# A hand-written step order and its engine assignment exchanged for another, in a polysketch attention kernel with a multiplicative feed-forward part

## The chip, the cores and the metric

The kernel runs on one core of one Trainium2 chip. The metric is the device time of one execution in microseconds; the time of a kernel is the median of several runs. Short names of the engines: PE is TensorE (its weight loads are PEld), DVE is VectorE, ACT is ScalarE, POOL is GpSimd, SP is SyncE, which issues nearly all transfers.

## The reference

Polysketch attention, linear in the length of the sequence, and behind it a feed-forward part without a non-linearity other than a product:

```python
def phi(x):                                   # x: (4, 4, 1088, 32), S1, S2: (8, 32)
    a = np.einsum('rd,bhsd->bhsr', S1, x)
    b = np.einsum('rd,bhsd->bhsr', S2, x)
    return np.einsum('bhsi,bhsj->bhsij', a, b).reshape(*x.shape[:-1], 64)
q_p, k_p = phi(q), phi(k)
kv = np.einsum('bhsf,bhsd->bhfd', k_p, v)
z = np.sum(k_p, axis=2)
num = np.einsum('bhsf,bhfd->bhsd', q_p, kv)
den = np.einsum('bhsf,bhf->bhs', q_p, z)[..., None] + 1e-06
x = (num / den).astype(np.float32)            # -> (4352 tokens, 128)
h = (x @ w1) * (x @ w2) @ w3                  # w1, w2: (128, 1024), w3: (1024, 1024)
out = (h @ w_out).astype(np.float32)          # w_out: (1024, 128)
```

The inputs come as 64-bit floats, of which the kernel takes the words apart itself.

## The kernel before

The work is cut into about a thousand small steps, each a function under a name; one step issues one or a few instructions. A string `ORDER` lists all names. The entry function calls the steps in that order and chains, on every engine, each instruction behind the one before it. So each engine runs its instructions exactly in the order of the string, and waits where an input of the next one isn't there. Nothing overtakes on an engine. Steps whose names end in `.load` are transfers; each bulk one also waits until the fourth one before it has landed.

Four more tables belong to it. `SLOTS` names for every tile the buffer it gets: `b` are the 8 PSUM banks, `m`, `l`, `s` and others are buffers in SBUF. A tile waits until the one that had its buffer before is read for the last time. `POOL` is the set of steps that run on GpSimd instead of DVE, and `CPV` the set of copies out of PSUM that run on DVE instead of ACT. `WARM` gives the sizes of the filler steps `warm0` to `warm11`: matmuls on a tile of zeros (L255, tile idle_ps) that compute nothing.

The names of the steps that the text speaks of:

- `s.*` prepare the sketch matrices (`s.Pp`: four 32x32 operations on P, L409 to L412).
- `w0.*`, `w1.*` convert the two halves of w1 and w2 to 32-bit values; `w3` to `w10` are rows of w3, `f0` to `f7` fold w3 with w_out into one matrix, once for all tokens (L534).
- `k0` to `k3` are the keys of the four batches. `lead` and `rest` split k into two summands, tile kk (L214 and L651). `gram0` to `gram4` multiply k with itself on PE (L659, tile ps_g); `G*`, `T*`, `N*` make a scaling from it; `kp` is the feature map (L677), `kv*` the sums over the sequence.
- `q0` to `q3` are the halves of the queries of batches 0 and 1, `q4` and `q6` all of batches 2 and 3, `qr` the rest of 64 positions. A q part ends in `xc`, `xT` (L1274, L1291): the attention's output, transposed, which the feed-forward part reads.
- `g0.0a` to `g3.7o` are the feed-forward part of q0 to q3: for each of 8 chunks of d_ff two products `a`, `b` on PE (L1799, L1809, 128x512), a copy `c`, a product `m` on DVE (L1815), and the output product `o` (L1835). `gr.*` is the same for qr.
- `h4.*` and `h6.*` are the feed-forward part of q4 and q6 by a seven-product scheme: products of 64 rows (L1673), `h4.0a1` to `h4.3b7`, those with `a` on rows 0 to 63 of the array, those with `b` on rows 64 to 127 (`tile_position`). Sums `m11` to `m22`, `T1` to `T4` follow, then products `P1` to `P7` (L1759) and their sums `k1` to `k9`.
- `oT`, `oS`, `st` transpose, finish and store the output; `gr.st1` is the last store.

PE has products of the feed-forward part to do for most of the time, and the steps of attention lie between them in the string. Until q0's xT is ready, PE has attention work only.

## Time and profile before

| | before |
|---|---|
| time, median of 3 runs | 245.06 us (244.8, 245.06, 246.78) |
| span of the profiled execution | 244.1 us |
| PE, DVE, POOL, ACT busy | 97%, 85%, 66%, 51% |
| granted clock of PE | full in all 40 slices |
| transfers | 22.06 MB, 90 GB/s in the mean |

The page gives the busy time of each engine over the whole span, then in 40 slices. For a kernel whose one engine is busy 97% of the span, the shares tell little: what matters is the stretches in which that engine is not busy. The span of 244.1 us is the only time known of the profiled execution itself; the median of the runs is 0.96 us above it.

### The profile page before, as it was taken

What the parts mean: (1) busy time and instruction counts of PE and PEld (TensorE: products, weight loads), DVE (VectorE), ACT (ScalarE), POOL (GpSimd) and SP (SyncE); (2) the same over time, 40 slices, a digit from 0 to 9 for tenths busy, and PEclk for the clock granted to TensorE, in tenths of its full rate; (3) what the DMA queues carried; (4) which work ended last, traced back from release to release, by engine and by line L of the source; (5) the groups of instructions that cost most, each with busy time, mean ns of one, the idle gap of its engine ahead of it and who ended that gap; (6) DMA issues with size and microseconds to landing.
All of it is one profiled execution on the core that took longest, in us unless ns stands there. A gap on an engine that the chain in (4) does not pass through costs nothing.

```text
span 244.1 us, 6745 instructions
## 1 busy us (share of the span) xinstructions
PE 236.2 (97%) x2724; PEld 129.8 (53%) x2724; DVE 206.7 (85%) x421; ACT 123.5 (51%) x246; POOL 161.9 (66%) x203
## 2 busy tenths in 40 slices
PE   8998999899999999999999999999999999999994
PEld 5887454545545646766566444444443354463363
DVE  2876988999899998997899878498989789999792
ACT  3976957675666764593012914355651164730010
POOL 4576658344856998764583889929999425883670
PEclk9999999999999999999999999999999999999999
DMA  7959797078859897200000000360000000000054
GB/s 201 265 143 325 181 227 190 6 197 224 220 141 251 188 217 190 59 1 3 3 0 0 4 0 3 59 113 3 1 0 0 0 3 0 0 1 3 12 90 93
DMA packets 31935, 22.06 MB, mean 90 GB/s; under 512 B 21280, under 2 KB 26528, under 8 KB 31904
## 3 DMA queue, kind: packets, MB, share of 16 engines
q1 hardware_dynamic: 31360, 21.11, 35.1%
q8 instruction: 21, 0.34, 0.6%
q10 hardware_dynamic: 544, 0.52, 0.6%
q14 instruction: 10, 0.08, 0.1%
HBM read 19.40 MB, written 2.23 MB: 89 GB/s over the span
## 4 chain that ended last, share of the span: by engine, by line
PE 87%; DMA 5%; ACT 2%; POOL 2%; DVE 1%; issue 1%; POOLq 0%; SPq 0%
PE b_ps L1809 12%; PE ps_o L1835 12%; PE ps_X L1673 11%; PE a_ps L1799 11%; PE ps_o L1759 10%; PE ps_w3o L534 6%; PE ps_Y L1673 6%; PE ps_Z L1673 3%; PE ps_g L659 2%; PE ps_x L1527 2%; PE ps_ac L1374 2%; DMA qh<-in_q_dram 2%; DMA k<-in_k_dram 2%; PE ps_or L1824 2%; POOL ph L1208 1%; PE idle_ps L255 1%
## 5 line engine op out<-in xcount | busy, mean ns | idle before, releaser
L1673 PE MATMUL ps_X<-xd,wv 64*128 64x512 f32 x112 | 36.3, 593 | 0.0
L1799 PE MATMUL a_ps<-xT,w 128*128 128x512 f32 (+1 forms) x80 | 36.1, 562 | 0.0
L1809 PE MATMUL b_ps<-xT,w 128*128 128x512 f32 (+1 forms) x80 | 35.6, 555 | 0.0
L1804 ACT COPY ffa<-a_ps 128x512 f32<-128x512 f32 (+1 forms) x38 | 20.1, 540 | 29.2 <-PE a_ps L1799 26.7
L1707 POOL TENSOR_TENSOR hc<-hc 128x512 f32<-128x512 f32 x16 | 20.7, 1304 | 15.7 <-DVE hc L1685 15.5
L1835 PE MATMUL ps_o<-ab,w3o 128*128 128x512 f32 x64 | 29.6, 600 | 0.0
L1680 ACT COPY hc<-ps_X 128x512 f32<-128x512 f32 x38 | 21.3, 590 | 16.1 <-PE ps_X L1673 12.9
L1815 DVE TENSOR_TENSOR ab<-ffa,b_ps 128x512 f32<-128x512 f32 (+1 forms) x40 | 23.9, 623 | 4.9 <-PE b_ps L1809 4.1
L501 POOL TENSOR_TENSOR w3c<-w3c,cv_m 128x512 int32<-128x512 int32 x16 | 21.2, 1344 | 4.2 <-DVE w3c L495 4.1
L1673 PEld LDWEIGHTS ps_X<-xd,wv 64*128 64x128 f32 x112 | 14.9, 186 | 13.1 <-issue 10.9
L1799 PEld LDWEIGHTS a_ps<-xT,w 128*128 128x128 f32 x80 | 14.1, 189 | 13.9 <-issue 8.8
L1809 PEld LDWEIGHTS b_ps<-xT,w 128*128 128x128 f32 x80 | 14.4, 190 | 13.1 <-issue 8.1
L1673 PE MATMUL ps_Y<-xd,wv 64*128 64x512 f32 x48 | 19.7, 594 | 0.0
L1835 PEld LDWEIGHTS ps_o<-ab,w3o 128*128 128x128 f32 x64 | 11.6, 190 | 13.4 <-issue 13.0
L534 PEld LDWEIGHTS ps_w3o<-wo,w3T 128*128 128x128 f32 x128 | 15.3, 192 | 2.4 <-issue 2.4
L534 PE MATMUL ps_w3o<-wo,w3T 128*128 128x128 f32 x128 | 15.7, 276 | 0.0
L1759 PE MATMUL ps_o<-hc,w3o 128*64 128x512 f32 x32 | 15.1, 595 | 0.0
L1759 PE MATMUL ps_o<-tt,ws 128*64 128x512 f32 x32 | 13.7, 594 | 0.0
L1680 ACT COPY hc<-ps_Y 128x512 f32<-128x512 f32 x14 | 8.1, 592 | 9.7 <-PE ps_Y L1673 6.6
L263 ACT ACTIVATE cv_c<-raw 128x1024 f32<-128x1024 f32 (+1 forms) x13 | 13.0, 1014 | 0.0
L1540 ACT COPY xd<-ps_x 64x256 f32<-64x256 f32 x24 | 8.8, 367 | 7.2 <-PE ps_o L1835 6.8
L1497 POOL COPY nz<-nz 32x8 f32<-32x8 f32 x32 | 11.1, 347 | 1.4
(347 smaller groups left out, 593.0 us busy)
## 6 DMA issues: line engine op xcount, KB each, us to landing
raw<-in_moe_w_dram SPq DMA_DIRECT2D x32, 256.0 KB, 5.0
qh<-in_q_dram SPq DMA_DIRECT2D x4, 544.0 KB, 4.5
raw<-in_moe_w_dram SPq DMA_DIRECT2D x4, 512.0 KB, 5.8
out_dram<-oT SPq DMA_DIRECT2D x32, 64.0 KB, 2.0
k<-in_k_dram SPq DMA_DIRECT2D x3, 512.0 KB, 5.1
v<-in_v_dram SPq DMA_DIRECT2D x2, 512.0 KB, 6.1
kh<-in_k_dram SPq DMA_DIRECT2D x8, 128.0 KB, 3.6
raw<-in_moe_w_out_dram SPq DMA_DIRECT2D x4, 256.0 KB, 5.0
```

The source lines that it names most:

```text
L263: act.activation(dst, hi.bitcast(F32), ACT.Prelu, scale=2.0 ** -112, alpha=-2.0 ** 32)
L501: pool.tensor_tensor(d, d, x["m"][:, i * 512:(i + 1) * 512], ALU.add)
L534: pe.matmul(t["o"], w3T[ko][:, c], wo[:, c], start=c == 0, stop=c == NC - 1)
L1673: pe.matmul(x[bank], stat(j, u)[:, i * 128:(i + 1) * 128], rows(j, u), start=new, stop=True, tile_position=(u * 64, 0), skip_group_check=True)
L1680: cp(n(y))(x[k], x[bank])
L1707: on(f"h{g}.{i}m{k}").tensor_mul(both[0][k], both[0][k], both[1][k])
L1759: pe.matmul(acc_o[bank][half[0]:half[1]], w(i), x(i), start=n == 1, stop=n == (2 if j == 3 else 4), tile_position=(0, half[0]), skip_group ...
L1799: pe.matmul(x["a"][:, :w], w_of(0, c), xT[g][:, c0:c0 + w], start=True, stop=True)
L1804: cp(f"g{g}.{c}{su}c")(x["s"][:, :w], x["a"][:, :w])
L1809: pe.matmul(x["b"][:, :w], w_of(1, c), xT[g][:, c0:c0 + w], start=True, stop=True)
L1815: dve.tensor_mul(ab_sb[g, c][:, c0:c0 + w], x["s"][:, :w], x["b"][:, :w])
L1835: pe.matmul(o_ps[g], w3o[:, c], ab_sb[g, c], start=n == 1, stop=n == NC)
```

## The change

The first 60 steps of the string stay as they are (up to `q0.sma`). Everything behind them stands in another order. `SLOTS` has other buffers for most tiles, so that the new order finds them free. The set `POOL` grows from 90 to 95 steps: 31 leave it for DVE, 36 enter it. `CPV` grows from 17 to 20: 19 copies go from ACT to DVE and 13 leave DVE for ACT (among these q0.xc0 and q0.xc1). The sizes of the fillers stay. All instructions are the same, on data of the same shapes; only the engine of these steps, the buffers and the order differ. The core of the diff:

```diff
 POOL = set("""
...
-    h4.2m12 h4.2m22 h4.3m11 h4.s2 h4.s4 h6.0T2 h6.0m11 h6.0m12 h6.0m22 h6.1T2 h6.1T3 h6.1m11 h6.1m12
-    h6.1m22 h6.2T1 h6.2T4 h6.2m11 h6.3T3 h6.3m11 h6.s1 h6.s2 h6.s4 k0.Nf k0.Nh k0.Nr k0.kp1 k1.Nr
-    k1.kp1 k2.kp0 k2.kp1 k2.rest0 k3.kp0 k3.kp1 q0.al q0.p01 q0.phi1 q0.sca q1.al q1.bs q1.p12
-    q1.phi q1.sca q2.bs q2.p2 q2.phi0 q2.sc q2.sl q3.al q3.bs q3.p01 q3.p12 q3.p2 q3.phi0 q3.sc
+    h6.s2 h6.s3 h6.s4 k0.Nf k0.Nh k1.Nr k1.kp1 k3.Nr k3.kp0 k3.rest0 q0.al q0.phi1 q0.scy q1.bs
+    q1.p12 q1.p2 q1.sca q1.scy q2.al q2.bs q2.p01 q2.p12 q2.phi0 q2.sc q2.sl q3.al q3.p01 q3.p12
...
 ORDER = """
...
-h4.0ah h4.1bc h4.0b6 h4.0be h4.0a6 h4.s4 h4.0ae h4.0bh h4.1a6 h4.1b6 h4.1be h4.0b3 h4.1ad h4.1ae h4.0a5 h4.0ad g1.st
+h4.0ad h4.0bh h4.1ad h4.0b6 h4.0ae h4.0a3 h4.0be v.4 h4.1b6 h4.0a2 h4.0b5 h4.1ac h4.0bd h4.0b7 h4.0af h4.0a7 h4.1a6
```

The two lines of `ORDER` are a piece of h4's products; in the second, products of the same half (the letter behind the dot's digit) stand next to each other at some places, such as h4.0b5 and h4.0b7.

DVE from `q0.sma` on (the reduction into s_ga, the last step that both orders share), before:

```order
L1074 TENSOR_REDUCE s_ga<-ps_a 128x16
L201 SCALAR_TENSOR_TENSOR s_t<-s_ga,ps_a 128x128
L204 SCALAR_TENSOR_TENSOR s_hla<-s_ga,s_t 128x128
L651 TENSOR_TENSOR kk<-k,kk 128x4x160
L1050 STREAM_TRANSPOSE s_bs<-ps_c 128x256
L1097 TENSOR_TENSOR s_hla<-ps_a,s_hla 128x128
L217 TENSOR_REDUCE G_g<-ps_g 128x1
```

And now, P2a to P2s being s.Pp, krT kr1.kT, kp k0.kp1:

```order
L1074 TENSOR_REDUCE s_ga<-ps_a 128x16
L409 TENSOR_SCALAR P2a<-P_c,P_g 32x32
L410 TENSOR_TENSOR P2b<-P_c,P2a 32x32
L411 TENSOR_TENSOR P2b<-P2b,P_c 32x32
L412 TENSOR_TENSOR P2s<-P2a,P2b 32x32
L651 TENSOR_TENSOR kk<-k,kk 128x4x160
L201 SCALAR_TENSOR_TENSOR s_t<-s_ga,ps_a 128x128
L825 COPY krT<-ps_krt 128x128
L677 TENSOR_TENSOR kp<-kab 128x1024
L204 SCALAR_TENSOR_TENSOR s_hla<-s_ga,s_t 128x128
L217 TENSOR_REDUCE G_g<-ps_g 128x1
```

Six more instructions stand ahead of the reduction into G_g, and two (s_bs and the sum into s_hla) stand behind it.

DVE ahead of q0's xT (L1291), before:

```order
L1189 TENSOR_REDUCE s_d<-s_pr 128x2x16
L1194 SCALAR_TENSOR_TENSOR s_rc<-s_d 128x16
L1198 RECIPROCAL s_rc<-s_rc 128x16
L466 TENSOR_SCALAR w_81<-cv_c 128x2x256
L1274 COPY xc<-ps_xt 128x256 x2
L1291 TENSOR_TENSOR xT<-xc,ps_xs 128x256 x2
```

And now, s_hl being q1.sh and q1.sl, qT the transposition q2.tr:

```order
L1189 TENSOR_REDUCE s_d<-s_pr 128x2x16
L1194 SCALAR_TENSOR_TENSOR s_rc<-s_d 128x16
L1198 RECIPROCAL s_rc<-s_rc 128x16
L466 TENSOR_SCALAR w_81<-cv_c 128x2x256
L204 SCALAR_TENSOR_TENSOR s_hl<-s_g,s_t_540 128x2x128
L1333 STREAM_TRANSPOSE qT<-qh 128x512
L1157 TENSOR_TENSOR s_hl<-ps_a,s_hl 128x2x128
L1291 TENSOR_TENSOR xT<-xc,ps_xs 128x256 x2
```

The copies xc went to ACT; three steps of q1 and q2 came in front. Further ahead q1.sm, q1.st and q1.Ct did too.

DVE between k2's lead (L214) and k2's rest (L651), which is new here (it was on POOL):

```order
L214 TENSOR_SCALAR kk<-k,k_g 128x1152
L1208 TENSOR_TENSOR ph<-s_al,s_bs 128x1024
L201 SCALAR_TENSOR_TENSOR G_t<-G_g,ps_g 128x32
L720 STREAM_TRANSPOSE kT<-kh 128x512
L1815 TENSOR_TENSOR ab<-ffa,b_ps 128x512
L204 SCALAR_TENSOR_TENSOR G_a<-G_g,G_t 128x32
L651 TENSOR_TENSOR kk<-k,kk 128x1152
```

Before, DVE had at this place:

```order
L214 TENSOR_SCALAR kk<-k,k_g 128x1152
L1333 STREAM_TRANSPOSE qT<-qh 128x512
L1815 TENSOR_TENSOR ab<-ffa,b_ps 128x512
L904 TENSOR_TENSOR T_p<-ps_T,T_p 32x32
```

Both the feature map ph of q1 (q1.phi) and the rest of k2 moved from POOL to DVE, and k2's rest has five instructions between it and the lead that it reads.

Four fillers moved as well: warm8 and warm9 (one matmul each) stood ahead of k0's N products and stand behind k3.Nr and f1.o now; warm11 (two) stood just behind the first of these and stands ahead of h4's products now.

More of the change, by code (lines that the diff above doesn't have):

```diff
@@ L143 @@
+h6.2P4 h6.3P3 h6.0P3 gr.6a g5.oT gr.7o0 h6.k3 gr.2o0 h6.k4 gr.4b h6.k5 gr.4a gr.4c gr.5o0 g5.oS h6.k7 h6.k6 gr.3o0
+h6.k8 gr.1b gr.6c g6.oT g5.st gr.3o1 gr.2o1 gr.6b gr.0b g6.oS h6.k9 gr.4m g7.oT gr.6m gr.4o1 gr.5o1 g6.st gr.6o1
+gr.6o0 gr.4o0 gr.1m gr.1o0 g7.oS gr.0m gr.7o1 gr.0o1 gr.1o1 gr.0o0 gr.oT0 gr.oT1 g7.st gr.st1
 """
```

159 lines of the change are left out of this document (79 added, 80 removed).

## The prediction

> **What bounds the kernel now.** I read the page first, to see which engine is full; then the times by stretch, to see where that engine is not full; then its waits there.
>
> ```profile
> PE 236.2 (97%) x2724; PEld 129.8 (53%) x2724; DVE 206.7 (85%) x421; ACT 123.5 (51%) x246; POOL 161.9 (66%) x203
> ...
> PE 87%; DMA 5%; ACT 2%; POOL 2%; DVE 1%; issue 1%; POOLq 0%; SPq 0%
> ...
> L255 PE MATMUL idle_ps<-zeros 128*128 128x256 bf16 x53 | 9.1, 315 | 1.0 <-DVE zeros L229 1.0
> ```
>
> TensorE (PE) is busy 97% of the span of 244.1 us and makes up 87% of the chain that ended last. VectorE (DVE) follows at 85%. Some of PE's busy time is no work: L255 issues the fillers, matmuls on zeros, 53 of them.
>
> ```profile
> 1.00:27.42 26.42, 24.48 (x506) 19.60 (x507) 17.90 (x57) 18.90 (x46) 14.81 (x47) 1.00 0.78 230
> 27.42:50.00 22.58, 21.18 (x456) 11.48 (x457) 19.96 (x51) 15.05 (x30) 14.50 (x18) 1.00 0.61 148
> 50.00:240.60 190.60, 190.56 (x1763) 98.75 (x1761) 168.48 (x315) 89.27 (x171) 132.18 (x135) 1.00 0.28 65
> ```
>
> The columns are the stretch, its length, then busy us of PE, PEld, DVE, ACT and POOL, and last PE's clock, the DMA share and GB/s. From 50 us to PE's end at 240.6 PE has 0.04 us free, at full clock. So order and engines behind 50 us can hardly gain anything; they can only break this. All that can be won lies ahead of 50 us. Adding up PE's work there from start to start, without fillers, I find 16.3 us ahead of the first product of the feed-forward part, which starts here:
>
> ```profile
> 27.42 1.96 PE L1799 MATMUL a_ps<-xT,w 128*128 128x512 f32 x4
> ```
>
> So 27.42 - 16.3 = 11.1 us from the span's start were idle or filler. Behind it only two holes of weight follow. One is 0.41 us from start to start, ahead of this transposition of ph; the other stands in the chain in order of time:
>
> ```profile
> 38.37 0.33 PE L1246 MATMUL ps_ph<-ident,ph 128*128 128x128 f32 x1 [0.24 <-POOL ph L1208]
> ```
> ```profile
> 44.27 1.56 PE ps_g L659 x75
> 45.83 1.16 issue
> ...
> 71.22 3.43 PE b_ps L1809 x8
> ```
>
> In the latter an instruction waits for nothing the profile shows, in the middle of k2's Gram products: 1.16 us there, 1.33 from start to start. I read it as waiting for the next block of instructions: a dense run of short matmuls uses them up faster than they arrive. Thus PE's loss is 11.1 + 0.4 + 1.3 = **12.85 us**, all ahead of 47 us, and the rest of 240.6 is 227.75 us of work, which the change leaves as it is (same instructions). In such a kernel the forecast is one question: how large is the loss after the change?
>
> **First place: when q0's xT is ready.** The first product needs xT, made on DVE by the last of these rows:
>
> ```profile
> 14.91 0.19 DVE L217 TENSOR_REDUCE G_g<-ps_g 128x1 f32<-128x32 f32 x1 [1.35 <-PE ps_g L659]
> ...
> 16.63 1.21 DVE L677 TENSOR_TENSOR kp<-kab 128x1024 f32<-128x1024 f32 x1
> ...
> 18.96 0.16 DVE L937 TENSOR_TENSOR RC<-RC,ps_Nr 128x8 f32<-128x8 f32 x1 [0.41 <-PE ps_Nr L912]
> ...
> 19.64 0.78 DVE L1208 TENSOR_TENSOR ph<-s_al,s_bs 128x512 f32<-128x512 f32 x1
> ...
> 23.20 0.32 DVE L1068 STREAM_TRANSPOSE ay_C<-ps_cy 128x128 f32<-128x128 f32 x1 [1.38 <-PE ps_cy L1030]
> ...
> 25.71 0.74 DVE L1274 COPY xc<-ps_xt 128x256 f32<-128x256 f32 x2
> 26.48 0.79 DVE L1291 TENSOR_TENSOR xT<-xc,ps_xs 128x256 f32<-128x256 f32 x2
> ```
>
> From 11.0 (q0.sma's first row) to xT's end at 27.28 DVE idles 1.35 + 0.41 + 1.38 = 3.14 us; without idling it would end at 24.1. The changed order puts 49 instead of 39 instructions there. What comes in front of xT costs, by these rows:
>
> ```profile
> 27.19 0.42 DVE L1137 TENSOR_REDUCE s_g<-ps_a 128x32 f32<-128x256 f32 x1
> 27.64 0.42 DVE L201 SCALAR_TENSOR_TENSOR s_t<-s_g,ps_a 128x256 f32<-128x256 f32 x1
> 27.98 0.57 DVE L1130 STREAM_TRANSPOSE ay_C<-ps_c 128x384 f32<-128x384 f32 x1
> 28.48 0.41 DVE L204 SCALAR_TENSOR_TENSOR s_hl<-s_g,s_t 128x256 f32<-128x256 f32 x1
> 28.92 0.42 DVE L1157 TENSOR_TENSOR s_hl<-ps_a,s_hl 128x256 f32<-128x256 f32 x1
> 29.26 1.35 DVE L651 TENSOR_TENSOR kk<-k,kk 128x1152 f32<-128x1152 f32 x1
> ...
> 32.32 0.70 DVE L1333 STREAM_TRANSPOSE qT<-qh 128x512 f32<-128x512 f32 x1
> 32.95 0.38 DVE L1176 TENSOR_TENSOR s_pr<-s_hl 128x256 f32<-128x256 f32 x1
> ```
>
> q1's five steps .42 + .42 + .57 + .41 + .42 = 2.24; q2's transposition 0.70; the second kp (the row of 1.21 above, on POOL until now) 1.21; q0.p01 from POOL 0.38; kr1.kT from ACT 0.25 (the row below); q0.sca 0.29 (the 128x128 form; estimate from the half-width rows here); s.Pp, four 32x32 operations, 0.8 (estimate: four times the 0.16 to 0.19 of DVE's smallest rows above). Sum 5.87.
>
> ```profile
> 22.26 0.25 ACT L824 COPY krT<-ps_krt 128x128 f32<-128x128 f32 x1
> ```
>
> Away go the two copies xc (0.74), q0.scy 0.29 and one w1 conversion 0.42, some 1.5. Net **+4.3**, so xT is ready at 28.4 at the earliest. The added work fills holes first: at 14.9 DVE is still in it, so the hole of 1.35 goes. I take 0.5 us of idling to remain: 28.9, the first product 1.5 us late. PE's work ahead of it is the same 16.3, so the loss there is 28.9 - 16.3 = 12.6 instead of 11.1, but with the fillers' order changed none of the later 1.7 is bound to return: after the change at least 3.5 us of PE work lie between dense Gram blocks instead of 2.5, so the wait of 1.33 may vanish. By this place alone the time stays within 0.3 us.
>
> **Second place: k2's Gram products.** They need kk of k2, made here:
>
> ```profile
> 36.36 1.95 POOL L1208 TENSOR_TENSOR ph<-s_al,s_bs 128x1024 f32<-128x1024 f32 x1
> 38.27 1.27 POOL L470 TENSOR_TENSOR w<-w,cv_m 128x512 int32<-128x512 int32 x1
> 40.45 2.62 POOL L651 TENSOR_TENSOR kk<-k,kk 128x1152 f32<-128x1152 f32 x1 [0.91 <-DVE kk L214]
> ```
>
> Both ph (q1.phi) and kk (k2.rest0) come to DVE, where kk takes 1.35 (row above) instead of 2.62, and ph about 1.4 (estimate between 0.78 for half the width, q0.phi0, and POOL's 1.95). But DVE does them in turn behind all else. From xT to kk's end the changed order gives DVE 22 instructions; by their rows they come to 11.3 us, of which 1.35 are k1's kk, 1.4 ph, 0.70 a transposition, 0.69 a gating product, 1.35 this kk. So kk ends at 28.4 + 11.3 = 39.7 at the earliest, and with an estimated 1.0 us of idling at 40.7. At the same time the Gram products move up: PE has 27.3 us of work ahead of them (16.3 plus nine products of 0.86, two passes of the 0.43 that b_ps shows above, k1's Gram products of 1.7 and small ones) instead of 32.75. With today's loss PE is there at 12.85 + 27.3 = 40.15. It waits 0.55 us for DVE, and the loss becomes 40.7 - 27.3 = **13.4**, +0.55. What bounds it: no idling gives 12.4 (-0.45); the full 3.14 us of idling of before gives 15.5 (+2.65). I take 1.0 since DVE is late rather than early, and such an engine finds its inputs ready. The next waits for DVE (k1.Nb, k1.Ta) come out at 11.8 to 12.1 without idling; past 50 us the distance grows.
>
> **Fillers.** Four of the 53 move behind 47 us, where PE is full: one each after k3.Nr and f1.o, two ahead of h4's products. Their price is from the last run of fillers:
>
> ```profile
> 17.36 0.61 PE L255 MATMUL idle_ps<-zeros 128*128 128x256 bf16 x4
> ```
>
> Taking off the 0.27 of one, three more cost 0.34, or 0.11 each; alone between other matmuls at most the 0.27. Four: 0.45 to 1.1; I take **+0.45**.
>
> **Half-array products.** h4 and h6 put products of 64 rows on the array's halves, a and b. Before, a and b alternate strictly. After, up to three of one half stand in a row.
>
> ```profile
> 74.58:76.28 1.70, 1.70 (x145) 1.70 (x144) 1.70 (x4) 1.64 (x2) 0.35 (x1) 1.00 1.10 233
> 155.71:182.50 26.79, 26.79 (x125) 12.58 (x124) 22.95 (x37) 15.09 (x28) 21.79 (x20) 1.00 0.24 40
> ```
>
> The second row has 125 matmuls in 26.79 us, 0.214 each, half of the 0.43 that one on the full array takes. So the halves overlap fully. If a pass can wait for its half while the other half runs on, with three or more waiting, the runs cost at most 4 passes of 0.427, +1.7; with six, 0. k3's Gram products, 72 in 1.70 us on quarters of the array, need at least three waiting, else they would take 2.4. I take 0, bound +1.7.
>
> A rule of the Trainium skill, "TensorE: Matmul & The Clock Gate", section "Part 3: Packing small matmuls — row/col tiling", speaks against any such order: matmuls start and end in program order. By it I estimate 9 passes more than before for the change, +3.8 us. It would also have made the stretch above 77 passes of 0.427, 32.9 us, and the row shows 26.8: the trace disagrees.
>
> **Tail.** gr.st1 is issued when its last copy ends:
>
> ```profile
> 237.85 2.74 SPq L1556 DMA_DIRECT2D out_dram<-oT  x5
> ...
> 240.60 0.29 DVE L1858 COPY oT<-ps_or 128x128 f32<-128x128 f32 x1 [1.41 <-PE ps_or L1824]
> 240.95 0.62 SPq L1562 DMA_DIRECT2D out_dram<-oT  x1
> ```
>
> g7's store, four issues of about 0.5 us (first row), stands directly ahead of it on SP both times. Counted from h6.k9 it is issued 5.0 us later either way, and PE has 6.6 instead of 5.4 us of work behind the last seven-product sum, so k9 comes earlier against the end. I take 0; if DVE lags, up to +1.
>
> **Sum.** In the profile 244.1 + 0.55 + 0.45 = 245.1; the median stands 0.96 above the span, so 245.06 + 1.0 = **246.1 us**. The other moves (POOL 161.9, ACT 123.5) stay behind PE everywhere I looked, each by over 5 us, and their buffers come free in time.
>
> **Rivals.** (a) DVE idles behind PE as before, 3.14 us: 245.06 + 2.65 + 0.45 = 248.2, slower. The place is k2.rest0; it decides once DVE idles over 2.4 us between 11 and 40. For it: every hole of before was DVE waiting for PE, and PE starts late too. Chance 0.18. (b) The halves stall: +1.7 makes 247.8; by strict order 249.9 (of that 0.02). Chance 0.10. (c) Nothing is lost: DVE never idles, the wait of 1.33 goes, loss 12.4, 245.06 - 0.45 + 0.45 = 245.1; the order matters to PE nowhere. It is also the result if the change merely shuffles covered work. Chance 0.25. (d) A real gain of over 2.45 us needs a loss under 9.95 with the fillers, below the bound of 12.4 that DVE's sum sets; only a sum wrong by 2 us allows it. Chance 0.05. My forecast keeps 0.42.
>
> About 1% is what a measurement of this kernel can tell from no change: 242.6 and 247.5. Slower is (a) and most of (b): 0.26; faster 0.05; within 0.69. The likeliest alone spans 245.4 to 246.9. The range takes in (c) and most of (a) and (b): 244.4 to 249.0.
>
> **What would show it.** Step one: the first a_ps of 512 columns starts at 28.9 (28.4 to 30) instead of 27.42. Step two: PE waits at L659 around 41 for DVE's kk at L651, and POOL has no kk of k2. No wait of over 1 us for "issue" near 45. Four idle_ps behind 47 us. From 50 us PE is full, and a stretch of half products still runs at 0.214 a matmul. I am wrong if a second stretch with PE idle appears behind 50 us, from a buffer that comes free late, or if PE's loss is under 12.

## The result, and the profile after

| | before | after |
|---|---|---|
| time, median | 245.92 us (4 runs beside after's) | 252.3 us (252.91, 250.77, 252.89, 251.71) |
| ratio, 95% interval | | 1.027 [1.0214, 1.0326]: slower |
| span of the profiled execution | 244.1 us | 251.1 us (its own time is 252.91 us) |
| end of PE's last product | 240.56 us | 246.77 us |
| issue of the last store (gr.st1) | 240.95 us | 247.95 us |

Time minus span is 1.7 to 2.0 us in every run shown here. So the 0.96 us of the text above set a span beside the median of other runs; by an estimate from this difference, the profiled execution of before was one of about 245.9 us. The forecast was 246.1 us and no measurable change; the measured cost is 2.7%, outside the range. Two runs further down, 278.98 us with two steps back on GpSimd (granted clock 0.85) and 1341.7 us of the second mixture, stood far above the others of their kernels; medians and ratios leave them out.

First the page of after: its head, the engines' totals, the shares of the chain, and the group of the half-array products.

```profile
span 251.1 us, 6775 instructions
...
PE 241.4 (96%) x2724; PEld 146.7 (58%) x2724; DVE 208.8 (83%) x425; ACT 119.1 (47%) x240; POOL 154.7 (62%) x205
...
PE 87%; DVE 7%; DMA 2%; issue 1%; POOL 0%; ACT 0%; DVEq 0%
...
L1673 PE MATMUL ps_X<-xd,wv 64*128 64x512 f32 x112 | 43.1, 596 | 0.0
```

PE runs the same 2724 instructions and is "busy" 5.2 us longer (236.2 before); its weight loads 16.9 us longer (129.8). The group of L1673 was `36.3, 593` in before: one matmul still has 596 ns, yet together they cover 6.8 us more. Matmuls that used to lie over one another now lie beside one another. That alone is no loss yet, as the starts below show.

Next the windows of after, cut as the prediction cut them (columns as there; 30.67 is where the first product of 512 columns starts, 27.42 before).

```profile
1.00:30.67 29.67, 25.78 (x503) 20.77 (x503) 20.69 (x67) 20.10 (x51) 11.35 (x45) 0.94 0.85 239
30.67:50.00 19.33, 18.98 (x368) 10.20 (x368) 18.66 (x42) 15.65 (x29) 10.62 (x13) 1.00 0.83 216
50.00:246.80 196.80, 196.60 (x1866) 115.70 (x1855) 169.21 (x316) 82.80 (x161) 132.28 (x144) 1.00 0.23 53
```

Behind 50 us PE has 0.2 us free in 196.8. By busy time nothing is lost there, and this is the trap of this case: a stretch with work on one half of the array and none on the other counts as full.

**Where the 7.0 us of span went.** PE's end is 6.2 us later, and the last store another 0.8.

*Half-array products: +3.8.* There are 168 of them (112 on halves of the rows, 56 P products on halves of the columns), two matmuls each. The row of before, then that of after, for the first 62 in a row, up to the first product that reads all 128 rows:

```profile
155.71:182.53 26.82, 26.82 (x125) 12.58 (x125) 22.98 (x37) 15.12 (x28) 21.82 (x20) 1.00 0.24 40
```
```profile
158.49:187.56 29.07, 29.07 (x131) 20.01 (x125) 23.99 (x39) 15.18 (x32) 24.59 (x20) 1.00 0.22 37
```

The same 62 products took 29.07 instead of 26.82. The other stretches, from start to start: the 28 P products of h4 12.35 (12.17), 48 of h6 21.45 (20.80), the last 30 14.27 (13.53). The sum is 77.14 instead of 73.32. With both halves always at work a product would take 0.429 us, 72.07 for 168. I call what lies above it the **half loss**: 1.25 before, 5.07 after. How it looks, in the timelines of PE, before and then after:

```profile
156.67 0.59 PE L1673 MATMUL ps_X<-xd,w 64*128 64x512 f32 x1
156.68 0.59 PE L1673 MATMUL ps_X<-xd,wv 64*128 64x512 f32 x1
157.10 0.59 PE L1673 MATMUL ps_X<-xd,w 64*128 64x512 f32 x1
157.11 0.59 PE L1673 MATMUL ps_X<-xd,wv 64*128 64x512 f32 x1
```
```profile
158.49 1.12 PE L1673 MATMUL ps_X<-xd,w 64*128 64x512 f32 x2
159.56 0.67 PE L1673 MATMUL ps_Y<-xd,wv 64*128 64x512 f32 x1
...
160.07 0.59 PE L1673 MATMUL ps_Y<-xd,wv 64*128 64x512 f32 x1
160.30 0.59 PE L1673 MATMUL ps_X<-xd,wv 64*128 64x512 f32 x1
160.50 0.59 PE L1673 MATMUL ps_X<-xd,w 64*128 64x512 f32 x1
```

Before, the halves start together, 0.43 apart. After, the second product starts 1.07 us behind the first, which is on the same half, and 0.64 of the half loss lies there. From there the halves run out of step, 0.20 and 0.23 apart. No wait is shown in these rows: one half is at work. Being out of step costs nothing by itself. In the 7.29 us that follow, 17 products start, 0.429 us to each, which is the full pace:

```profile
160.07:167.36 7.29, 7.29 (x36) 5.87 (x34) 4.61 (x7) 4.72 (x9) 7.13 (x7) 1.00 0.72 120
```

The loss stands at some twenty places, where the next start comes later than that.

*Ahead of h4's products: +2.3.* Their first one starts at 158.49 instead of 155.71, 2.78 later; the four fillers that moved behind 47 us take 0.46 of it (0.11, 0.12, 0.12 and 0.11 from their starts to the next). The other products between and behind the stretches of half products took 0.4 less than before, which closes the sum: 2.3 + 0.46 + 3.8 - 0.4 = 6.2. PE's waits, then two pieces of the chain in order of time:

```profile
PE ps_a L1110 <- POOL Rh L943: 1.5, 1, 1.5
PE ps_kv L769 <- issue: 1.4, 1, 1.4
...
PE a_ps L1799 <- DVE xT L1291: 0.5, 1, 0.5
PE ps_g L659 <- DVE kk L651: 0.4, 1, 0.4
```
```profile
18.46 1.17 POOL Rh L943
...
21.22 1.40 issue
22.62 1.82 PE ps_kv L769 x59
```

PE waits 1.5 us for Rh (k0.Nh), a small operation on GpSimd, and 1.4 us for nothing the profile shows, in the middle of kv0 (before has such a wait at the same line, 0.9 us). Then these windows of one us follow (last columns PE's clock, DMA share, GB/s):

```profile
21.00:22.00 1.00, 0.22 (x11) 0.07 (x2) 0.97 (x3) 0.00 (x0) 1.00 (x2) 0.89 0.82 217
22.00:23.00 1.00, 0.38 (x17) 0.38 (x20) 0.60 (x3) 0.00 (x0) 0.49 (x1) 0.50 0.23 70
23.00:24.00 1.00, 1.00 (x48) 1.00 (x44) 0.00 (x0) 0.00 (x0) 0.00 (x0) 0.50 0.60 172
24.00:25.00 1.00, 1.00 (x41) 1.00 (x34) 0.00 (x0) 0.20 (x1) 0.00 (x0) 0.50 0.54 166
```

The granted clock is 0.50 for three us. DVE, which needs kv's and q's results, does nothing from 23 to 25.

*Tail: +0.8.* SP's issues, then DVE's rows:

```profile
238.49 9.36 SPq L1556 DMA_DIRECT2D out_dram<-oT  x12
247.95 0.62 SPq L1562 DMA_DIRECT2D out_dram<-oT  x1
```
```profile
241.78 0.71 DVE L1842 STREAM_TRANSPOSE oT<-oc 128x512 f32<-128x512 f32 x1
...
243.46 0.70 DVE L1842 STREAM_TRANSPOSE oT<-oc 128x512 f32<-128x512 f32 x1
...
246.59 0.29 DVE L1858 COPY oT<-ps_or 128x128 f32<-128x128 f32 x1 [1.29 <-PE ps_or L1824]
```

g6's transposition starts at 241.78, 5.0 us ahead of PE's end at 246.77, and g7's at 243.46, 3.3 ahead; before it was 234.47 and 236.65, 6.1 and 3.9 ahead. The stores of both, eight issues of about 0.5 us, fill SP from 243.7 on, so gr.st1 goes out 1.19 us behind PE's end, 0.39 before.

### The profile page after: what moved, and what is told of

It reads as the page before. It is cut to its first block, busy times and chain, and to the rows that moved or that the text cites. A ratio compares the mean times of both kernels' runs of the same rounds, so it can differ in the third digit from the quotient of the medians.

```text
span 251.1 us, 6775 instructions
## 1 busy us (share of the span) xinstructions
PE 241.4 (96%) x2724; PEld 146.7 (58%) x2724; DVE 208.8 (83%) x425; ACT 119.1 (47%) x240; POOL 154.7 (62%) x205
## 3 DMA queue, kind: packets, MB, share of 16 engines
HBM read 19.40 MB, written 2.23 MB: 86 GB/s over the span
## 4 chain that ended last, share of the span: by engine, by line
PE 87%; DVE 7%; DMA 2%; issue 1%; POOL 0%; ACT 0%; DVEq 0%
PE ps_X L1673 12%; PE b_ps L1809 11%; PE ps_o L1835 11%; PE a_ps L1799 11%; PE ps_o L1759 10%; PE ps_w3o L534 6%; PE ps_Y L1673 6%; PE ps_Z L1673 3%; PE ps_g L659 2%; PE ps_x L1527 2%; PE ps_ac L1374 2%; PE ps_kv L769 2%; DMA k<-in_k_dram 2%; PE ps_or L1824 1%; PE idle_ps L255 1%
## 5 line engine op out<-in xcount | busy, mean ns | idle before, releaser
L1673 PE MATMUL ps_X<-xd,wv 64*128 64x512 f32 x112 | 43.1, 596 | 0.0
L1799 PE MATMUL a_ps<-xT,w 128*128 128x512 f32 (+1 forms) x80 | 37.0, 565 | 0.5 <-DVE xT L1291 0.5
L501 POOL TENSOR_TENSOR w3c<-w3c,cv_m 128x512 int32<-128x512 int32 x16 | 21.3, 1341 | 17.5 <-DVE RC L936 10.2
L1680 ACT COPY hc<-ps_X 128x512 f32<-128x512 f32 x31 | 17.9, 590 | 21.6 <-PE ps_X L1673 11.8
L1673 PEld LDWEIGHTS ps_X<-xd,wv 64*128 64x128 f32 x112 | 18.9, 186 | 9.0 <-issue 4.6
L1673 PE MATMUL ps_Y<-xd,wv 64*128 64x512 f32 x48 | 21.9, 596 | 0.0
L1707 POOL TENSOR_TENSOR hc<-hc 128x512 f32<-128x512 f32 x15 | 19.6, 1321 | 3.1 <-DVE hc L1685 2.8
L1759 PE MATMUL ps_o<-hc,ws 128*64 128x512 f32 x32 | 15.6, 600 | 0.0
L1742 POOL TENSOR_TENSOR tt<-tt,hc 128x512 f32<-128x512 f32 x7 | 9.8, 1415 | 8.2 <-DVE tt L1732 7.5
L1509 POOL TENSOR_TENSOR ph<-s_al,s_bs 128x1024 f32<-128x1024 f32 (+1 forms) x7 | 13.2, 1887 | 0.9 <-DVE G_g L217 0.7
L263 ACT ACTIVATE cv_c<-raw 128x1024 f32<-128x1024 f32 (+1 forms) x13 | 13.1, 1018 | 0.0
```

The source lines that it names most:

```text
L501: pool.tensor_tensor(d, d, x["m"][:, i * 512:(i + 1) * 512], ALU.add)
L1509: on(nm(f"phi{u}")).tensor_mul(x, bview(s["al"][:, u * g], [[r, g], [1, r], [0, r]]), bview(s["bs"][:, u * g], [[r, g], [0, r], [1, r]]))
L1673: pe.matmul(x[bank], stat(j, u)[:, i * 128:(i + 1) * 128], rows(j, u), start=new, stop=True, tile_position=(u * 64, 0), skip_group_check=True)
L1680: cp(n(y))(x[k], x[bank])
L1707: on(f"h{g}.{i}m{k}").tensor_mul(both[0][k], both[0][k], both[1][k])
L1759: pe.matmul(acc_o[bank][half[0]:half[1]], w(i), x(i), start=n == 1, stop=n == (2 if j == 3 else 4), tile_position=(0, half[0]), skip_group ...
```

## The experiments

"Half loss" is as above, "first product" the start of the first a_ps of 512 columns. **My theory** after the result: the halves cost 3.8 us since products of one half stand in a row and the waiting room ahead of the array is short; the front costs through GpSimd's late Rh and the clock. **The rivals**: the halves wait for late copies and sums, or for their buffers, not for each other; the front costs through DVE's longer list.

### Halves taken in turns again

After, with 26 products moved so that the halves alternate nearly everywhere, for instance:

```diff
-qr.xT0 h6.s1 h4.0a5 h4.0b1 g2.oT h4.0ac h4.1a1 h4.0bc
+qr.xT0 h6.s1 h4.0b1 h4.0a5 g2.oT h4.0ac h4.0bc
```

> The changed kernel, with 26 of its half-array products moved by a few places so that the two halves alternate again (their running difference is at most 2, mostly 1, instead of 3); all else stays. Theory A: a pass that waits for its half holds up the passes behind it once more than two wait, so runs of one half leave the other half empty; counted by this rule, 9 passes of 0.427 us are lost in the changed kernel and 3 with alternating halves. The stretches of half products (h4, h6 and the P products) then take 2.5 us less than in the changed kernel (their sum there is 77.1 us), and the time is 2.5 us lower, near 249.8. Rival B: the half products wait for their inputs or run slower for another reason; then the same 3.8 us over the kernel before stay, and the time stays near 252.3.

Measured: 251.01 us, 1.0235 [1.0204, 1.0267]; half loss 4.71 instead of 5.07. Order alone gives back 0.36 of 3.8. At the start of h4 the loss grew from 0.64 to 0.86: h4.0b1, moved forward, met its bank before ACT's copy (L1549) had left it. In this profile PE also had nothing to do for 1.27 us behind 50 us, where ACT's copy ffa came late behind a transfer:

```profile
52.59 1.12 PE L1799 MATMUL a_ps<-xT,w 128*128 128x512 f32 x2 [1.27 <-ACT ffa L1804]
```

The profile of "g6's transposition earlier" has 1.01 us at the same place; after's has none.

### Runs of one half put into before

Before, with 17 products moved so that two to four (h4) and two and three (h6) of one half stand in a row:

```diff
-h4.1a3 h4.0a3 h4.1b5 h4.1bd h4.0b4 h4.0a4 h6.s2
+h4.0a3 h4.0a4 h4.1b5 h4.0b4 h4.1bd h6.s2
```

> The kernel before, with 17 half-array products moved so that runs arise: in h4 mostly two of one half in a row, in h6 two and three; all else stays. Theory A (more than two waiting passes block): by the same count 3 passes are lost in h4 and 4 in h6, 1.3 and 1.7 us, 3.0 in all; the time is near 248 to 249. Rival B (the order of halves is not what cost the time): 0, the time of the kernel before. If any run of two already blocked: 14 passes, 6.0 us.

Measured: 250.5 us, 1.0226 [1.0203, 1.0248]; half loss 6.85 instead of 1.25, 2.50 of it in h4 and 3.73 in h6. So order alone can cost more in the half products than the whole change does. The order in h4 has two runs of four, against the expectation's "mostly two". By the count that the test further down supports (four matmuls can wait), h4 and h6 lose two slots each, 1.7 us of the 5.6 added. The moved products also meet banks and sums at other times: PE's waits name DVE's hc with 0.65 and 0.68 us.

### Two steps back on GpSimd

After, with the front's largest additions to DVE taken away:

```diff
 POOL = set("""
+    s.Pp k0.kp1
```

> The changed kernel with two early steps put back on GpSimd: s.Pp (four 32x32 operations) and k0.kp1 (a 128x1024 product); all else stays. Theory: VectorE's load ahead of q0's xT sets the first feed-forward product; 2.0 us of work leave VectorE there, kp0 ends 2 us earlier, PE's wait ahead of q1.A0 shrinks, and the first full product starts near 28.7 instead of 30.67; the time falls by 1.5 to 2. Rival: a wait in PE's own order (the fetch of instructions in kv0, the low clock after it) sets it; then the product starts within 0.5 us of 30.67 and the time falls by under 0.5.

Measured: 251.09 us, 1.0262 [1.0232, 1.0291]; PE's wait for Rh is unchanged, 1.5 us. The first product came at 29.45 with the clock full, no earlier than in the profiles of after's front that kept the clock (27.7 to 28.6). So these two steps on DVE are not what costs. The reason stands in the rows of POOL, in before, after and this run:

```profile
18.43 0.24 POOL L943 TENSOR_TENSOR Rh<-RC,mask4n 128x32 bf16<-128x32 f32 x1
```
```profile
18.46 1.16 POOL L943 TENSOR_TENSOR Rh<-RC,mask4n 128x32 bf16<-128x32 f32 x1 [2.99 <-DVE RC L204]
```
```profile
20.13 1.16 POOL L944 TENSOR_TENSOR Rh<-RC,mask4n 128x32 bf16<-128x32 f32 x1 [2.99 <-DVE RC L205]
```

And of DVE beside it, after and this run:

```profile
18.30 1.22 DVE L677 TENSOR_TENSOR kp<-kab 128x1024 f32<-128x1024 f32 x1
```
```profile
19.97 1.22 DVE L678 TENSOR_TENSOR kp<-kab 128x1024 f32<-128x1024 f32 x1
```

Rh starts 0.16 us behind kp and ends 0.10 behind kp's end, both times: an operation of 0.24 us lasts as long as its large neighbour on DVE. That the neighbour holds it up is read from these rows; no run changed the neighbour alone.

### Fillers early

After, with warm8, warm9 and warm11 in front of q1.A0, and warm11 at 12 matmuls:

```diff
-k1.tr0 q0.al q1.A0 q0.A1
+k1.tr0 q0.al warm8 warm9 warm11 q1.A0 q0.A1
```

> The changed kernel with warm8, warm9 and warm11 moved from the full stretch to PE's wait ahead of q1.A0, and warm11 made 12 instead of 2 matmuls, so 14 fillers (1.5 us) stand in a wait of 1.68 us. Theory C: PE's idling at 18 to 19.7 and 21.2 to 22.6 us is what took the clock down to 0.5 from 22 to 25 us, and the fillers keep it up; kv1 to kvr then take 0.25 instead of 0.43 us each, the first full product starts 1 us earlier or more (near 29.5), and with the 4 fillers gone from the full stretch the time falls by 1.5 or more. Rival: the clock falls anyway, because of the second wait alone (the fetch); then only the 0.45 us of the four fillers is gained.

Measured: 251.71 us, 1.027 [1.0238, 1.0301]; clock 1.00 from 20 to 30 us, first product at 28.87. That says nothing of the fillers: the clock was full as well in seven other profiles with after's front and no such fillers. A wait of 1.01 us without a cause shown came at 44.15 instead.

### Before's front with after's back, buffers assigned anew

Before up to the last step ahead of h4's products, then after's order and engines; all buffers chosen anew (the one longest free).

```diff
 g3.oT h4.s3 h4.s4
+h4.0a1 h6.s1 h4.0a5 h4.0b1 g2.oT h4.0ac h4.1a1 h4.0bc o.S2 g2.st h4.1b1
```

> The order, engines and buffers of the kernel before up to the first half-array product of h4, and from there the order and engines of the changed kernel (its buffers chosen anew, each tile taking the one that came free first). Theory A: the changed kernel's loss lies mostly in its back part, 3.8 us in the half products by their order and 0.8 in the tail, so this takes 245.2 + 4.6 = 249.8. Rival D (the loss is in front of 60 us, by the fetch of instructions and the low clock): the time of before, 245 to 246.

Measured: 250.97 us, 1.0228 [1.0211, 1.0245]; half loss 5.94. Most of the cost follows the back.

### After's front with before's back, buffers assigned anew

```diff
 qr.x h4.s4 q6.xT3 qr.xT0 g1.oT
+h4.1a5 h4.0b5 h4.0bd h4.0a1 h4.0ac g2.oT h4.0b1 o.S2 h4.0bc h4.1a1 h4.1ac
```

> The other half: the changed kernel's order, engines and buffers up to its first half-array product of h4, and from there the order and engines of the kernel before (buffers chosen anew, as in the run beside it). Theory A: only the front's loss remains, 0.55 to 1.9 us, and 0.45 of late fillers: 246.2 to 247.6. Rival D: 249 or more. If both halves together come to more or less than the change, buffers or slots play a part.

Measured: 250.27 us, 1.0184 [1.0152, 1.0216]; half loss 3.60. Before's order with before's engines loses 2.35 more than in before, so the buffers matter too; that called for the two exact versions further down.

### Rh on DVE

```diff
 POOL = set("""
-    k0.Nh
```

> The changed kernel with k0.Nh (a 128x32 product, 0.24 us on GpSimd before, 1.17 us in the changed kernel, where it runs beside VectorE's kp0 of 1.22 us and ends 0.1 us behind it) put on VectorE, ahead of kp0. Theory E: GpSimd's small product is held up by the long one on VectorE, and PE waits for it at q1.A0 (1.68 us); on VectorE it takes 0.2, the wait falls to 0.8 or less, and the first full product comes 0.9 us earlier, counted from k0.gram4. Rival: the wait stays, because what makes Nh late is Na before it; then nothing changes in front.

Measured: 250.81 us, 1.0224 [1.0172, 1.0275]. PE's wait at q1.A0 fell from 1.5 to 0.6 us (now for ACT's cv_c), and from k0.gram4 to the first product it took 12.57 us instead of the 13.1 of two profiles with after's front and the full clock. The late Rh costs 0.5 us.

### The halves by themselves

Before, with a test appended behind all its work: products of ident, A on rows 0 to 63, B on rows 64 to 127, a full product between the groups.

```diff
+        for row in ("AB" * 6, "AABB" * 3, "AAABBB" * 2, "AAAABBBB", "A" * 6 + "B" * 6, "A" * 6):
+            for x in row:
...
+                pe.matmul(to[u], part, bview(part, [[0, 4], [1, 128]]), start=True, stop=True,
+                          tile_position=(u * 64, 0), skip_group_check=True)
+            full()
```

> The kernel before with a test behind its last store: products of 64 rows on the identity, 512 columns, two passes each, with no input to wait for, in blocks of 12 (the fourth 8): ABABABABABAB, AABBAABBAABB, AAABBBAAABBB, AAAABBBB, AAAAAABBBBBB, AAAAAA, with one full-array product between blocks. Twelve products take 12 x 0.43 = 5.1 us if the halves overlap fully and 10.2 if never. Theory A (a pass that waits for its half blocks the ones behind it when more than two wait): AB 5.1, AABB 5.6 to 6, AAABBB 6.4 to 7, AAAABBBB 5 (of 3.4), AAAAAABBBBBB 9. Rival (a longer queue, six or more): 5.1 in the first three and 3.4 to 3.8 in the fourth. Strict order of all ends: AABB near 7.7 and more. What it says of the cost of one run is the cost beside which the kernels' 3.8 us stand.

Measured, PE's timeline (L1891 the test, two matmuls to a product; L1884 the full ones):

```profile
241.45 5.42 PE L1891 MATMUL ps_half<-ident 64*128 64x512 f32 x24
246.80 1.98 PE L1884 MATMUL ps_half<-ident 128*128 128x512 f32 x4
248.71 5.53 PE L1891 MATMUL ps_half<-ident 64*128 64x512 f32 x24
254.17 1.98 PE L1884 MATMUL ps_half<-ident 128*128 128x512 f32 x4
256.08 6.38 PE L1891 MATMUL ps_half<-ident 64*128 64x512 f32 x24
262.39 1.98 PE L1884 MATMUL ps_half<-ident 128*128 128x512 f32 x4
264.31 5.52 PE L1891 MATMUL ps_half<-ident 64*128 64x512 f32 x16
269.76 1.98 PE L1884 MATMUL ps_half<-ident 128*128 128x512 f32 x4
271.68 8.96 PE L1891 MATMUL ps_half<-ident 64*128 64x512 f32 x24
280.56 1.98 PE L1884 MATMUL ps_half<-ident 128*128 128x512 f32 x4
```

From start to start the 24 matmuls took 5.35 us in turns, 5.46 as AABB, 6.31 as AAABBB and 8.88 as six and six. Less the same 0.22 at the seam, and in slots of 0.4275: 12, 12.25, 14.25, 20.25. The 16 matmuls of AAAABBBB took 5.45, 12.25 slots. A model in which four matmuls can wait for their half, and every matmul passes through one of these places, gives 12, 12, 14, 20 and, for AAAABBBB, 12. So runs of two are free, and runs of three in a row cost. A product of the free half starts ahead of waiting ones of the other, so "nothing overtakes on an engine" does not hold for PE's halves. The rule of the Trainium skill that the prediction weighed ("TensorE: Matmul & The Clock Gate", section "Part 3: Packing small matmuls — row/col tiling"; matmuls start and end in program order) is contradicted here too: the B's of AABB could not start beside the A's by it, and I count 19 slots for AABB by that rule as an estimate, where 12.25 were taken. Counting after's order by this model, it loses 4 slots, 1.7 us, and before's none. That is the bound the prediction named; 2.1 us of the 3.8 it does not explain.

### After's front, before's back with its own buffers

As two experiments above, but from the seam on every tile has the buffer it has in before.

```diff
 qr.x h4.s4 q6.xT3 qr.xT0 g1.oT
+h4.1a5 h4.0b5 h4.0bd h4.0a1 h4.0ac g2.oT h4.0b1 o.S2 h4.0bc h4.1a1 h4.1ac
```

> As the run with the changed front and the back of before, but with the buffers of before in the back too (one for one, only renamed to fit those in use at the seam). In the earlier run the back lost 2.35 us more in the half products than the kernel before although its products stood in the same order, and only its buffers were new. Theory F (buffers): a bank that comes free late holds up a product and then all behind it; with the old buffers the half products fall back to before's loss, 1.3 us over the ideal, plus at most 0.6 at the seam, and the time is 2 lower than there, near 248. Rival: the seam (late copies on ACT) or the front makes the loss; then it stays near 250.3.

Measured: 247.98 us, 1.0129 [1.0088, 1.017]; half loss 2.23, of which 0.66 at the first two products behind the seam, first product at 28.13. The group of the half products on the page:

```profile
L1672 PE MATMUL ps_X<-xd,wv 64*128 64x512 f32 x112 | 36.9, 594 | 0.0
```

The group covers 36.9 us, where before has 36.3 and after 43.1. The buffers alone made 3.60 into 2.23.

### Before's front, after's back with its own buffers

```diff
 g3.oT h4.s3 h4.s4
+h4.0a1 h6.s1 h4.0a5 h4.0b1 g2.oT h4.0ac h4.1a1 h4.0bc o.S2 g2.st h4.1b1
```

> The front of the kernel before and the changed kernel's back with the changed kernel's own buffers (renamed at the seam). Theory A: the loss in the half products is the changed kernel's, 5.1 us over the ideal or, if the 0.64 at its first product came from its front, 4.5; with the tail's 0.8 the time is 245.3 + 3.3 to 3.8 + 0.8, 249.4 to 249.9. If much of the 3.8 came from the seam between its own front and back, the half products come under 3.5 and the time under 248.7.

Measured: 250.16 us, 1.021 [1.0156, 1.0264]; half loss 4.89; the last store 1.19 us behind PE's end, as in after.

```profile
L1674 PE MATMUL ps_X<-xd,wv 64*128 64x512 f32 x112 | 43.4, 598 | 0.0
```

This pair settles where the time is: the back as a whole (order, engines, buffers) brings 3.6 of the half loss's 3.8 and the whole tail. The front with before's back costs 1.3%, with 1.0 us of added half loss in it, more than half of that at the seam; the back alone costs 2.1%.

### A mixture

After's front and before's back as above, with the fillers early (sizes as in after), Rh on DVE, and two output products behind qr.x:

```diff
-qr.pT0 v.2 warm11 g0.oT q6.xT0 g1.7o g2.7o q6.xT1 q6.xT2 g2.5o qr.x h4.s4
+qr.pT0 v.2 g0.oT q6.xT0 g1.7o q6.xT1 q6.xT2 qr.x g2.7o g2.5o h4.s4
```

> A version meant to beat both: the changed front and before's back as in the first kernel here, and three edits: warm8, warm9 and warm11 back ahead of q1.A0, where PE waits anyway (0.45 us out of the full stretch); k0.Nh on VectorE (took 0.9 off PE's wait there); two output products g2.7o and g2.5o behind qr.x, so that PE has work while ACT copies q6's xT (takes away most of the 0.6 at the seam). If the front without a late instruction block loses 11.5 instead of 12.85 us, as the runs counted from k0.gram4 show, this takes 245.3 - 1.35 + 0.3 = 244.3; if a late block comes in (1.4), it takes 245.5 to 246.

Measured: 247.68 us, 1.0095 [1.0051, 1.0139]; half loss 1.38. The seam's loss went, but qr.x, moved forward, now waits 0.25 and 0.45 us for the copies xd.

### Runs of three removed by moving products back only

After, 16 products moved to later places, so that none meets its bank earlier than in after.

```diff
-qr.xT0 h6.s1 h4.0a5 h4.0b1 g2.oT h4.0ac h4.1a1 h4.0bc g1.oT o.S2 g2.st h4.1b1
+qr.xT0 h6.s1 h4.0b1 h4.0a5 g2.oT h4.0ac h4.0bc g1.oT o.S2 g2.st h4.1b1
```

> The changed kernel with 16 half-array products moved a few places back (none forward, so that none meets an input that isn't there yet), which takes the runs of three away. The test with products alone gave the rule: four passes can wait for their half; by it the changed kernel loses 4 passes, 1.7 us, and this one none. Theory A with that rule: the half products lose 3.4 instead of 5.1 us over the ideal, and the time falls by 1.7. Rival F (the rest, and maybe all, is banks and inputs that come late): they stay within 0.5 of 5.1.

Measured: 250.44 us, 1.0217 [1.0183, 1.0251]; half loss 5.01. One run of three is left, in h6; by the count with four places none of the order's runs cost anything now, and still nothing was gained: my theory in its first form has fallen. What the queue would have cost is hidden behind something else, or moved there.

### Two banks exchanged

After, with other PSUM banks for h4.0a5 and h4.0b1, the two products at the start of h4 that began 0.15 and 0.05 us behind the ends of ACT's copies out of their banks. The steps g2.oT and g1.oT also moved ahead of qr.xT0.

```diff
-h4.0a1 qr.xT0 h6.s1 h4.0a5 h4.0b1 g2.oT h4.0ac h4.1a1 h4.0bc g1.oT o.S2
+h4.0a1 g2.oT g1.oT qr.xT0 h6.s1 h4.0a5 h4.0b1 h4.0ac h4.1a1 h4.0bc o.S2
```

> The changed kernel with the PSUM banks of the first h4 products exchanged (h4.0a5 takes bank 0 instead of 4, h4.0b1 bank 6 instead of 3; the names exchanged from there on), all else in its order. In the changed kernel h4.0b1 starts 0.01 us after ACT's last copy out of qr.x, which had its bank, and 0.64 us of the half products' loss lies there. Theory F (banks): the stop goes, h4's loss falls from 1.95 to 1.3 us over the ideal, and h6 and P stay at 1.58, 0.34 and 1.2. Rival: the loss only moves to the next product; then their sum stays at 5.1.

Measured: 250.73 us, 1.0229 [1.0201, 1.0258]; h4's part 1.76 instead of 1.95, sum 4.89. (The 0.01 us of the expectation belongs to another matmul; the product's load began 0.05 us behind the first of the four copies.) One wait taken away gives 0.2.

### Banks, runs and copies together

The two edits above and five copies of h4's products back on ACT:

```diff
 CPV = set("""
-    h4.0be h4.1bc h4.2bc h4.3ai h4.3bc
```

> The changed kernel with all three suspects of the half products taken away at once: the two banks as in the run beside it, the 16 products moved back so that no runs of three of one half are left, and the five copies of h4 that the change put on VectorE (h4.0be, 1bc, 2bc, 3ai, 3bc) back on ACT. If each costs on its own what the others hide (a run that is gone shows a bank that is late), the loss over the ideal falls from 5.1 to 3 us or less, and the time by 2. Rival: what remains is order in general, near 5.

Measured: 250.97 us, 1.0232 [1.0203, 1.026]; half loss 5.33, with losses of 0.98 at h4.3b6 and 0.53 at h4.0b7. PE's row at the first of these:

```profile
176.06 0.69 PE L1673 MATMUL ps_X<-xd,wv 64*128 64x512 f32 x1 [0.48 <-ACT hc L1680]
```

So the three edits did not simply bring nothing. The start of h4 now loses 0.10, where the run with the 16 moves alone lost 0.95. But both places above belong to products that wait for a copy put back on ACT: h4.3b6 began 0.05 us behind the end of h4.3bc, h4.0b7 0.05 behind h4.0be. In after, with h4.3bc on DVE, h4.3b6 also began 0.05 behind that copy's end, and some 0.3 us are lost around it. At this place a late copy is shown as the cause.

### g6's transposition earlier

```diff
-h6.k6 gr.3o0 h6.k8 gr.1b gr.6c g6.oT g5.st
+h6.k6 gr.3o0 g6.oT h6.k8 gr.1b gr.6c g5.st
```

> The changed kernel with one step moved: g6.oT on VectorE ahead of h6.k8 instead of behind it (as the kernel before has it). g6's four stores and g7's four are issued one after another on SP, half a microsecond each, and gr.st1 waits behind them. Theory G: the tail is this queue; g6.st starts 0.7 us earlier, gr.st1 too, and the time falls by 0.7. Rival: g7's or gr's last copies set the end; then 0.

Measured: 250.5 us, 1.0216 [1.0188, 1.0245]. SP's issues:

```profile
237.90 7.99 SPq L1556 DMA_DIRECT2D out_dram<-oT  x10
245.99 0.62 SPq L1562 DMA_DIRECT2D out_dram<-oT  x1
```

PE ends at 245.29, so the last store goes out 0.70 us behind it instead of 1.19. The tail's cause, a late transposition and SP's queue of stores behind it, is shown for 0.5 of its 0.8 us, by the move of the last store against PE's end.

### A second mixture

After's front, before's back with its buffers, fillers early, Rh on DVE, other banks at the seam, and:

```diff
-qr.x h4.s4 q6.xT3 qr.xT0 g1.oT h4.1a5
+qr.x g1.oT h4.s4 q6.xT3 qr.xT0 h4.1a5
```

> The second attempt at a version that beats both: the changed front and before's back with its own buffers, the four late fillers back in PE's wait at q1.A0, k0.Nh on VectorE, and at the seam other banks for the first h4 products, with g1.oT ahead of h4.s4. Against the first attempt g2.7o and g2.5o stay where they were; there qr.x came without other work ahead and lost 1.0 us. The half products at before's 1.3 us over the ideal, no late fillers, the front's loss 11.5 to 12 instead of 12.85: 1 us under the kernel before, 244.3. With a late instruction block it is the time of before, 245.3 to 246.

Measured: 246.5 us, 1.0063 [1.0033, 1.0092]; half loss 1.56. With the late fillers, the wait for Rh and most of the seam's loss removed, the front is still 0.6% slower than before's, where the expectation had a gain. No version beat before.

### After's engines in before's order

Before, with after's sets POOL and CPV for the steps of h4 and h6 (33 steps change between DVE and GpSimd, 16 between DVE and ACT):

```diff
 CPV = set("""
-    h4.1ac h4.1ad h6.1bc h6.2ad
+    h4.0be h4.1bc h4.2bc h4.3ai h4.3bc h4.k1 h6.0ae h6.1ac h6.1be h6.2bd h6.3ae h6.k1
```

> The kernel before, order and buffers untouched, but the steps of h4 and h6 on the changed kernel's engines (of the sums and T steps 13 leave GpSimd and 20 come to it; of the copies 4 go from VectorE to ACT and 12 the other way). Theory H (engines): copies and sums that come later by their engine hold up the products; the half products' loss rises from 1.25 to 3 us or more over the ideal. Theory A' (order): it stays under 2, and what it costs is at most the tail.

Measured: 263.06 us, 1.0721 [1.068, 1.0762]; half loss 18.7. PE's waits name the steps that changed engines:

```profile
PE ps_o L1759 <- DVE hc L1680: 3.0, 1, 3.0
PE ps_X L1673 <- POOL wv L1600: 1.5, 1, 1.5
```

L1680 are the copies of CPV; before's list of PE's waits has neither row. (In the whole change 16 copies leave DVE for ACT, not 13 as said above: 17 - 16 + 19 = 20.)

### Before's engines in after's order

The same exchange the other way round, in after:

```diff
 CPV = set("""
-    h4.0be h4.1bc h4.2bc h4.3ai h4.3bc h4.k1 h6.0ae h6.1ac h6.1be h6.2bd h6.3ae h6.k1
+    h4.1ac h4.1ad h6.1bc h6.2ad
```

> The changed kernel, order and buffers untouched, with the steps of h4 and h6 on the engines of before. Theory H (engines): the half products' loss falls from 5.1 to 3 us or less over the ideal, and the time by 2 or more. Theory A' (order): it stays at 4.5 or more; the order of the products among each other and among their copies is what costs, whichever engine does the copies.

Measured: 260.17 us, 1.0616 [1.0574, 1.0658]; half loss 11.73. So the new engines are no fault by themselves: they belong to the new order and buffers, as the old ones to the old.

## Why the prediction was wrong

- **"Half-array products … I take 0, bound +1.7": this step failed.** It measured +3.8. The bound counted one mechanism, the queue ahead of the array, and the bound had that one right: four matmuls wait, after's order would lose 1.7. The term itself was taken at 0, which needed six places, without evidence for six. ("Before, a and b alternate strictly" is wrong, too: 40 times two products of one half stand in a row in before's order; since runs of two are free, the sum does not change.) Rival (b) named the right place with a chance of 0.10; its variant with strict order came out at 3.8 by coincidence, since strict order does not hold in the test of the halves. What I never priced is that a half product must also wait for a free bank, which a copy or a sum on ACT, DVE or POOL frees, and that such a wait of one half is invisible in busy time. The sentence that the other moves "stay behind PE everywhere I looked, each by over 5 us, and their buffers come free in time" was an argument from totals (POOL 161.9, ACT 123.5 of 244.1). h4.0b1's load began 0.05 us behind the copy that freed its bank, and h4.3b6 waited for the copy h4.3bc. Of the 22 places with loss in after, 11 are followed within two products by a load or matmul that started at most 0.06 us behind what it waited for, and they hold 2.2 of the 5.07 us; in before it is one place of 14. Such starts also occur at 40 of the 146 other places without loss, so this points to late copies and sums but does not price them. Order alone is worth up to 5.6 (runs put into before), buffers alone 1.1 to 1.4 (3.60 against 2.23, 5.94 against 4.89), engines alone 17.5 in before's order. These don't add up: each piece of after's back fits the others. The back as a package costs the 3.6 to 3.8; that is shown. How it is shared among runs, banks and copies is not settled: taking the runs away, exchanging two banks, and both with five copies back on ACT, left the sum at 4.9 to 5.3, with losses at other places.
- **"First place", "Second place": right in size, with one event missing.** In seven of the eight other profiles with exactly this front the first product started at 27.7 to 28.6 (forecast 28.9, range 28.4 to 30), k2's Gram products at 39.2 to 40.1 (forecast 40.7): a loss of 11.9 to 12.8 where I had 13.4 and rival (c) 12.4. They waited 0.4 us for DVE's kk (forecast 0.55), and the wait of 1.33 among them is gone. The profile of before was itself a late one: in five others with its front the first product started at 26.2 to 27.7. By the medians, 26.8 and 28.1, the change makes it 1.3 us late (forecast 1.5). The sum behind the forecast has a small slip, net +4.3 where its terms give +4.4. In the profiled run, and in the eighth (before's engines in after's order, first product at 30.32), there were a wait without a cause shown at 21.2 and then three us at half clock; in the profiled run the loss there is 42.20 - 27.3 = 14.9. Rival (a)'s figure of 15.5 was nearly reached, by PE's own stalls and not by its mechanism. Rh stands in none of the prediction's sums; what DVE does beside it cost 0.5.
- **Fillers: +0.45** is right: from their starts to the next ones' the four took 0.46 us in after.
- **"Tail. I take 0; if DVE lags, up to +1": DVE lagged, +0.8.** The bound held. The prediction compared distances from h6.k9 and did not ask where g6's transposition stands on DVE.
- **"The median stands 0.96 above the span": 1.7 to 2.0 in all runs.** A span must be set beside its own execution's time. It shifts the forecast by no more than 0.9 us.
- **The signs.** "From 50 us PE is full" held in after's profile, and 4.6 us were lost there and behind it all the same. ("A second stretch with PE idle behind 50 us" came in two other profiles of after's front, 1.27 and 1.01 us at 51.) The test that would have told was the last one, "a stretch of half products still runs at 0.214 a matmul": 29.07 / 124 is 0.234.

## What to carry to other kernels

When an engine's sub-arrays run side by side, measure a stretch by products per us from start to start, and look for the places where the next start comes late; the busy share stays full while half the array waits, and halves out of step are no loss by themselves. This full engine was not robust: its order, buffers and engine sets are one design (the engine sets of h4 and h6 alone, exchanged in before, cost 7%), and where all three change, "its partners are idle half the time" is no argument; look at the slack of each buffer, from the reader's end to the next writer's start. Before an operation is priced from its row, look at what its neighbour was doing in that row and will be doing in the new place.

## What the runs showed of the hardware

- Four matmuls can wait for a busy half of the array while the other half goes on. In the test of the halves runs of two were free, runs of three and of six cost (12.25, 14.25 and 20.25 slots for 24 matmuls, against 12 in turns).
- In after the clock fell to 0.50 at 21.8, in the second of two waits of PE, 1.5 and 1.4 us, that lay 1.6 us apart (18.2 to 22.6), and stayed there until 25.2. The Trainium skill ("TensorE: Matmul & The Clock Gate", section "Part 1: The HAM clock gate (the "warmup" mystery)") gives an idle window of about 3.4 us as the cause; no single gap here is that long. Before's engines in after's order had the same two waits, 1.5 and 0.6 us, and 0.50 from 22.0 to 25.4; after's engines in before's order had 0.50 from 193.7 to 197.1, begun within one wait of 3.0 us. Seven profiles of after's front with the first wait alone kept 1.00. Four executions of after had mean clocks of .992, .998, .991 and .996, and the two lowest took 252.9 us where the others took 250.8 and 251.7, so it varies from run to run of one kernel.
- Waits of PE with no cause shown stand in dense runs of short matmuls, and their place goes with the front. All six profiles with before's front have one in k2's Gram products, 0.87 to 1.16 us, between 44.6 and 46.1. After's front has none there; two of its nine profiles have one at 21.2, 1.40 and 0.65 us. That it is instructions arriving late is my reading, not shown.
- A 128x32 operation on GpSimd of 0.24 us took 1.16 beside a DVE operation on 128x1024, and ended 0.10 us behind it, twice.
- SP takes 0.50 us (median of 32) for each store it issues, so the row of eight from 243.7 on held back the last one until 247.95.
